# A transformer block on one core: the written-out order of its 4663 steps, and the engine of 320 of them, replaced

## The chip, the core and the metric

The kernel runs on one NeuronCore of a Trainium2 chip. Five engines work side by side, each through its own queue, in the order in which the program issues: TensorE (PE in the profile; its weight loads are PEld) multiplies matrices into PSUM, VectorE (DVE) and ScalarE (ACT) work elementwise on SBUF and PSUM, GpSimd (POOL) works elementwise on SBUF, and SyncE (SP) issues the transfers. [...] The metric is the device time of one execution in microseconds; the median of three runs is 767.39.

## The reference

One block with 2048 tokens of width 512, in float32: a layer normalization, causal attention with 32 heads of width 16 in a sliding window of 256, the output projection and the residual; then a layer normalization, a gated unit of inner width 1376 with a sigmoid gate, and the residual.

```python
q, k, v = qkv[0], qkv[1], qkv[2]                       # layernorm(x) @ wqkv
scores = jnp.einsum("bhqd,bhkd->bhqk", q, k) * (Dh ** -0.5)
mask = (idx[:, None] - idx[None, :] >= 0) & (idx[:, None] - idx[None, :] < W)
p = _softmax(jnp.where(mask[None, None], scores, -1e9), axis=-1)
o = jnp.einsum("bhqk,bhkd->bhqd", p, v)
h = x + o.transpose(0, 2, 1, 3).reshape(B, S, D) @ wo
z = _layernorm(h)
h2 = h + (_sigmoid(z @ w_gate) * (z @ w_up)) @ w_down
```

## The kernel before

**Numbers in two halves.** Every matrix product takes float16 operands, each split into a high half (a rounded copy) and a low half (the rest); a product is three matmuls, high by high, high by low, low by high. Making halves is most of the elementwise work: a high half is a copy (`copy`, L353 to L359, on ScalarE L355 or VectorE L357 and L359), a low half is a subtraction (`subtract`, L361 and L362, on GpSimd or VectorE). Weights are first scaled by a power of two found from their absolute maximum (`bound`, L364 to L369, then `scale`).

**Attention.** The tokens go in 8 blocks `b` of 256. For a block: two normalizations (`do_ln`, `normal`, L551 to L575), the projections (`do_qk`, `do_v`), copies of the keys and queries through DRAM into the stacked tiles `SK` and `SQ` (`do_keys` L677, `do_queries` L686), and for each of 8 groups `g` of four heads: scores for the row maxima (`do_s`, matmuls L740, maxima on VectorE L725), the maxima carried into two rows of `SQ` (`do_m`, L747 to L756), transposed scores with the maximum already subtracted (`do_st`, L794 to L805), their exponentials on ScalarE (L770), the masks on GpSimd (L778, L783), and products with the values (`do_pv`, L831). Then follow a transposition and an add (`do_o`, L861), the division and the output projection (`do_wo`, L873 to L899).

**The gated unit.** The tokens go in 8 pairs `p` of tiles, the inner width in three chunks `c` of 512, 512 and 352. Both sides of the products use a Strassen scheme: seven products in place of eight (`do_pair`, matmuls L1140), with sums taken of weights (`do_weights`, `do_split`, L988 to L1049 and L954, L956), of the normalized input (`do_ln2`, L1104 to L1123) and of the results. A pair's products are copied or added out of PSUM (`copied`, L357 and L355; `added`, L1161, L1163), go through the sigmoid (L1206) and the multiplication with the up side (`gated`, L1210), then four sums (`sum_`, L1224), and for four rows `r` of the hidden value a high half (`row`, through L355 or L357), a low half (through L362) and a transposition by DMA (L1240). The down products (`do_down`, L1317, L1323) read those rows; their results are added to the residual (L1288, L1300) and stored (L1294).

**What sets the order.** Each of these pieces is a Python generator. At each `yield` it names the engines that could do its next step, with a cost, and what must be done before; the step's instructions are issued when the generator goes on. `Planner.run` (L312) takes the next step from the list `ORDER` (L61 to L283): each number holds the root piece (the number without its low 7 bits), the piece among those which that root has added (the next 5 bits), and the engine (2 bits: 0 VectorE, 1 ScalarE, 2 GpSimd), used where the step leaves a choice. Costs are not used to choose anything here, nor is `Port`, which only marks steps within SBUF. So the list alone sets the order in which each engine's queue, SP's too, is filled, and which buffer of a ring (`RINGS`, L342) a step takes.

```python
        for code in ORDER:
            self.now = self.roots[code >> 7]
            item = self.now[code >> 2 & 31]
            costs, needs, *more = item[1]
            self.on = next(iter(costs)) if len(costs) == 1 else ENGINES[1 + (code & 3)]
```

Of the kernel before, what the change touches and what calls it, by code (L numbers as in the profile page):

```python
# [61 lines left out]
    3203, 3331, 771, 899, 1027, 1155, 7424, 2179, 2435, 7808, 7426, 1411, 7424, 641, 2051, 7810, 7424, 641, 1539, 7424, 1667, 7808, 641, 7427, 7808,  # L62
    3459, 7810, 1795, 641, 2307, 6658, 640, 7424, 3587, 643, 7811, 640, 2691, 3075, 641, 7808, 2947, 640, 641, 2819, 640, 641, 8323, 640, 641, 8323,
    640, 8323, 1280, 1281, 1921, 8323, 1921, 3715, 8195, 1281, 1280, 1920, 8323, 13056, 1921, 8323, 8323, 8323, 1280, 12672, 13058, 1283, 8321, 8195,
    8195, 1280, 8195, 3843, 12674, 8195, 2561, 8195, 1920, 7042, 8320, 8195, 8195, 1281, 1923, 8193, 1280, 8451, 2561, 2560, 8192, 1281, 1280, 1281,
    8579, 9219, 1280, 1281, 2561, 3971, 8451, 9219, 1280, 8451, 8835, 12672, 8579, 6018, 1920, 8835, 12673, 8451, 13056, 9219, 1921, 8451, 12672,
    8451, 4099, 1921, 8451, 18304, 8451, 8963, 8579, 1922, 8449, 8579, 8963, 2560, 8579, 1921, 8448, 8579, 8835, 6274, 8579, 1921, 13056, 8579, 8963,
    17920, 12675, 13058, 8577, 2563, 12673, 8576, 17922, 1920, 1921, 8707, 13059, 18306, 7683, 8707, 1920, 13057, 1920, 7683, 1921, 8067, 1920, 8067,
    1920, 7683, 17920, 49667, 8067, 23168, 17921, 4227, 8067, 17920, 8707, 7683, 50691, 8064, 7681, 51075, 2560, 9091, 17923, 18304, 13443, 8707,
    2561, 13443, 23552, 13443, 2561, 13443, 17921, 13443, 18304, 4355, 23554, 13443, 18304, 13443, 6402, 9091, 13443, 28416, 13571, 13441, 13571,  # L70
    6530, 9091, 13571, 10371, 10371, 13571, 10372, 10376, 6786, 13571, 13440, 13571, 13571, 13571, 10371, 10371, 10371, 13569, 10384, 23170, 13699,
    10388, 13699, 50688, 2562, 13699, 10380, 49665, 13699, 13568, 13699, 13699, 13699, 13699, 23168, 10371, 10371, 14467, 10371, 13697, 13827, 10392,
    10400, 13827, 4483, 9347, 10396, 13827, 9348, 14211, 13827, 13696, 9347, 9347, 9347, 13827, 14083, 9352, 13827, 9360, 10883, 14211, 9356, 13827,
    10884, 13827, 28800, 14211, 18307, 13825, 10883, 9347, 10883, 18305, 9364, 10888, 13824, 9347, 10883, 2561, 9368, 18691, 13955, 10892, 33664,
    18691, 2561, 14083, 9347, 18691, 23169, 18691, 14467, 9372, 9347, 18691, 10896, 23170, 13955, 18819, 9376, 9603, 18691, 14467, 9604, 10883, 10883,
    9603, 10900, 18691, 10904, 51203, 9608, 18691, 23552, 10883, 9603, 9603, 18689, 18819, 10908, 4611, 9616, 18819, 10883, 9612, 18819, 10912, 18819,
    18688, 18819, 18819, 13955, 9603, 9603, 18819, 9603, 50435, 2560, 2561, 18817, 18947, 51331, 18947, 9620, 9624, 14339, 18947, 9628, 51073, 18947,
    18816, 14083, 9603, 18947, 2561, 18947, 14339, 18947, 2562, 18947, 50179, 9632, 11139, 10115, 19075, 18945, 10116, 10115, 11140, 19075, 10120,
    13955, 2561, 6146, 11139, 11139, 19075, 11144, 11148, 19075, 2561, 18944, 11139, 7170, 10115, 19075, 10115, 11152, 19075, 10128, 19075, 14339,
    10124, 11139, 12931, 11156, 34048, 28418, 11139, 10115, 10115, 19075, 12931, 19073, 10136, 11160, 12931, 10132, 51201, 19072, 11139, 11139, 10115,  # L80
    12931, 11164, 11168, 10140, 10115, 13315, 12929, 10144, 50433, 12416, 11651, 11651, 11651, 13315, 11652, 11656, 12419, 11660, 11651, 13315, 11664,
    11907, 11907, 13315, 11908, 11912, 0, 11651, 11651, 11651, 18563, 13313, 11668, 11672, 12419, 11676, 51329, 11651, 11907, 11907, 11680, 23171,
    11916, 18563, 49411, 11920, 23169, 23552, 19203, 11907, 11907, 11907, 18563, 11928, 23554, 19203, 11924, 11932, 11907, 16387, 16387, 11936, 9475,
    9475, 18563, 33666, 16388, 9477, 9481, 16392, 16387, 28802, 16387, 18561, 9475, 16396, 16387, 9475, 6914, 9485, 12544, 16387, 9489, 23555, 16400,
    12547, 16404, 9475, 23553, 16387, 18179, 16408, 28416, 16387, 9497, 15619, 16412, 9475, 4739, 18179, 16416, 50177, 50051, 15620, 15619, 9731,
    24195, 9501, 12547, 15624, 15619, 15619, 24195, 9733, 15628, 28417, 15619, 9731, 15632, 9731, 24195, 19203, 9741, 15636, 15619, 24195, 9737,
    15640, 15619, 15619, 9731, 15644, 9731, 9745, 24195, 15648, 9753, 15363, 9750, 9731, 15364, 15363, 24195, 9757, 19331, 9506, 15368, 10243, 16899,
    15363, 24195, 10245, 16900, 9494, 10243, 10243, 15372, 9859, 16899, 10249, 16899, 9762, 24195, 10253, 38912, 50049, 15363, 10243, 28418, 10243,
    9859, 10257, 16908, 10265, 16904, 7298, 49409, 15376, 16899, 28800, 10243, 15363, 16912, 16899, 10269, 10499, 4867, 18179, 15380, 50819, 9857,
    16916, 10499, 10274, 15363, 18179, 19331, 10501, 15384, 10505, 9856, 10499, 15363, 18177, 16899, 14851, 10499, 15388, 10509, 24323, 28419, 10513,  # L90
    16920, 10499, 14852, 10518, 15363, 10499, 10521, 16899, 15392, 24323, 10262, 50563, 16924, 10525, 14851, 16899, 24323, 14856, 19331, 50817, 14851,
    11011, 16928, 10530, 24323, 19459, 11013, 14851, 14860, 24323, 39296, 11011, 10627, 14851, 19459, 11011, 14851, 10627, 11021, 28801, 49795, 14872,
    19459, 11017, 14864, 28802, 24193, 14868, 11011, 9987, 11011, 11025, 14851, 24192, 24323, 11033, 2562, 11011, 14876, 14851, 14595, 11037, 28803,
    11267, 14880, 24323, 14595, 11030, 14596, 11269, 11267, 14595, 10625, 14600, 11267, 24323, 34050, 11273, 14604, 14595, 14595, 11277, 11042, 14608,
    11267, 11281, 11267, 14612, 14595, 11289, 11267, 11286, 14616, 14595, 11395, 14595, 19587, 10624, 11293, 11779, 17155, 14620, 11781, 10755, 11779,
    11298, 14624, 11785, 11779, 17155, 24321, 17664, 17155, 11395, 17156, 11789, 17667, 49793, 24320, 17160, 11779, 17164, 17155, 24451, 11779, 11793,
    17168, 19843, 24451, 11801, 11779, 11798, 19844, 17155, 19843, 11805, 17172, 12035, 17155, 17667, 19848, 12037, 12035, 11810, 19843, 17176, 12041,
    12035, 17155, 19852, 12045, 19587, 12035, 17155, 17180, 12049, 12035, 19843, 11393, 17184, 12035, 12054, 19843, 19856, 12061, 19715, 19843, 19860,
    19843, 12057, 29443, 19715, 11392, 12163, 20867, 29443, 19864, 19715, 12066, 29443, 14723, 19587, 19843, 33664, 14723, 14725, 12163, 19868, 51843,
    33665, 19872, 4995, 14729, 20868, 20867, 50561, 14723, 20872, 20867, 14723, 14733, 29443, 20876, 20867, 14737, 20867, 29443, 20880, 14723, 12161,  # L100
    20884, 20867, 14742, 14723, 14749, 20867, 24067, 20892, 20867, 14753, 24067, 20888, 14979, 24067, 12160, 14981, 14758, 24067, 20896, 14979, 9986,
    16131, 24067, 44160, 14985, 14979, 14746, 16131, 11523, 29443, 14989, 14979, 16132, 16131, 29443, 16136, 14993, 14979, 16140, 16131, 16131, 15005,
    24067, 14998, 16144, 14979, 16148, 16131, 16131, 15009, 15491, 16152, 29443, 15002, 16156, 15493, 20099, 24067, 15014, 20100, 15491, 20099, 15491,
    10754, 20104, 20099, 16131, 24067, 16160, 20099, 12291, 15107, 15107, 24065, 29440, 20108, 17792, 15501, 20112, 17795, 15497, 29440, 51840, 20099,
    15105, 15491, 49539, 20116, 15491, 20099, 15505, 23939, 20120, 23939, 15517, 17795, 12288, 15491, 20099, 11520, 20611, 15521, 20611, 15747, 15514,
    20612, 23939, 49923, 15749, 20124, 15747, 15510, 23939, 20616, 15753, 20099, 15747, 20128, 20611, 20611, 15757, 15526, 15747, 20620, 23939, 15761,
    15104, 20611, 15747, 23939, 20624, 15773, 15747, 15770, 20611, 20628, 23939, 19203, 15777, 15766, 7552, 20611, 16259, 24064, 20611, 15875, 16259,
# [1392 lines left out]
```

## Time and profile before

| | |
|---|---|
| runs, us | 767.39, 767.2, 770.11 |
| median, us | 767.39 |
| the profiled execution: span, us | 769.3 |
| mean granted TensorE clock | 0.989 |
| busy PE, DVE, ACT, POOL, us | 729.6, 692.9, 436.9, 256.7 |
| instructions PE, DVE, ACT, POOL | 7030, 2067, 774, 319 |
| moved by DMA, MB | 118.57 |

The span runs from the first to the last instruction of the profiled execution. Busy time is the time in which at least one instruction of the engine was under way. A matmul's end is modelled and its latency counts, so PE can be busy throughout and still not be at its peak. The groups of instructions give count, busy time, mean duration of one, and the idle time of the engine just before them with what ended it.

### The profile page before, as it was taken

How to read it: one execution, taken by the hardware profiler on the slowest of the kernel's cores; microseconds unless marked ns; L12 is line 12 of the kernel's file. 1: busy time of each engine (PE TensorE's matmuls, PEld its weight loads, DVE VectorE, ACT ScalarE, POOL GpSimd, SP SyncE). 2: the span in 40 equal slices, each digit the busy share in tenths (PEclk: the TensorE clock that was granted, in tenths of full speed). 3: DMA queues.
4: the chain of work that ended last, by engine and by line, in shares of the span. 5: the costliest groups of instructions: out<-in, count | busy, mean ns of one | idle time of the engine just before them, and what ended most of it. 6: DMA issues, size and time to landing. Idle time of an engine off the chain costs nothing.

```text
span 769.3 us, 19057 instructions
## 1 busy us (share of the span) xinstructions
PE 729.6 (95%) x7030; PEld 502.0 (65%) x7030; DVE 692.9 (90%) x2067; ACT 436.9 (57%) x774; POOL 256.7 (33%) x319
## 2 busy tenths in 40 slices
PE   4899999999999999999999898699999999999997
PEld 3586678777686687686666554367565666666476
DVE  8999999978899999999998579999998989989973
ACT  5755788878688888798877667653222111121210
POOL 3333445535545466554757442240000000000000
PEclk9999999999999999999999999899999999999999
DMA  8586593886747989569587879455375665736535
GB/s 300 156 221 168 142 180 80 152 198 144 165 95 172 205 211 182 166 156 245 150 162 180 211 187 274 117 119 105 79 136 95 117 131 106 150 66 109 96 83 155
DMA packets 210318, 118.57 MB, mean 154 GB/s; under 512 B 174576, under 2 KB 183792, under 8 KB 210224
## 3 DMA queue, kind: packets, MB, share of 16 engines
q1 hardware_dynamic: 210224, 117.35, 67.9%
q8 instruction: 55, 0.90, 0.5%
q14 instruction: 39, 0.32, 0.2%
HBM read 43.65 MB, written 19.40 MB: 82 GB/s over the span
## 4 chain that ended last, share of the span: by engine, by line
PE 75%; DVE 11%; DMA 5%; issue 5%; ACT 3%; SPq 0%; DVEq 0%; ACTq 0%
PE mmp L402 18%; PE sp L1140 14%; PE mmp L1317 11%; PE pvp L831 7%; PE sp L740 6%; PE stp L1140 6%; PE pvp L1140 3%; PE stp L805 2%; PE stp L795 2%; DVE junk L725 2%; PE stp L794 1%; PE mmp L1323 1%; PE stp L796 1%; DMA oT<-whl 1%; ACT pa L770 1%
## 5 line engine op out<-in xcount | busy, mean ns | idle before, releaser
L725 DVE CUSTOM_DVE_ANT_0 junk<-sp,mask 128x320 uint8<-128x320 f32 (+4 forms) x512 | 215.4, 465 | 16.6 <-PE sp L740 14.0
L770 ACT ACTIVATE pa<-stp,kappa 128x512 f32<-128x512 f32 (+1 forms) x256 | 157.3, 645 | 48.0 <-PE stp L796 44.5
L1140 PEld LDWEIGHTS <-x 128*128 128x128 f16 x1008 | 98.3, 98 | 94.6 <-issue 10.1
L740 PE MATMUL sp<-SK,SQ 96*128 96x256 f16 (+3 forms) x960 | 129.6, 233 | 6.3 <-DVE mq L725 3.1
L402 PE MATMUL mmp<-xT,W 128*128 128x256 f16 x768 | 114.3, 281 | 3.3 <-DVE sq L661 1.7
L740 PEld LDWEIGHTS <-SQ 96*128 96x128 f16 x960 | 80.5, 97 | 30.9 <-issue 12.8
L1140 PE MATMUL sp<-W,x 128*128 128x512 f16 (+1 forms) x420 | 90.1, 351 | 6.5 <-ACT SQ L355 5.8
L770 ACT ACTIVATE pb<-stp,kappa 128x512 f32<-128x512 f32 x128 | 84.6, 685 | 19.7 <-PE stp L805 15.9
L402 PEld LDWEIGHTS <-W 128*128 128x128 f16 x768 | 71.4, 100 | 16.1 <-DVE W L539 2.9
L778 POOL TENSOR_SCALAR_AFFINE_SELECT pa<-pa 128x1024 f32<-128x1024 f32 x56 | 62.9, 1127 | 53.9 <-ACT pa L770 50.3
L831 PE MATMUL pvp<-pa,VT 128*17 128x128 f32 (+1 forms) x1408 | 62.5, 307 | 0.0
L795 PE MATMUL stp<-SQ,SK 100*128 100x256 f16 x224 | 60.2, 272 | 0.0
L563 POOL TENSOR_TENSOR rs<-rs,nhalf 128x1 f32<-128x1 f32 x32 | 20.2, 634 | 118.2 <-DVE rs L560 105.0
L783 POOL TENSOR_SCALAR_AFFINE_SELECT pa<-pa 128x512 f32<-128x512 f32 x64 | 42.6, 669 | 45.3 <-ACT pa L770 45.0
L1206 ACT ACTIVATE SQ<-sp,cg 128x512 f32<-128x512 f32 (+1 forms) x22 | 14.0, 636 | 76.6 <-PE sp L1140 76.3
L796 PE MATMUL stp<-SQ,SK 100*128 100x128 f16 x256 | 55.5, 219 | 0.7 <-ACT pb L770 0.4
L783 POOL TENSOR_SCALAR_AFFINE_SELECT pb<-pb 128x512 f32<-128x512 f32 x64 | 42.0, 658 | 42.6 <-ACT pb L770 40.1
L402 PE MATMUL mmp<-WO,oT 128*128 128x512 f16 x192 | 51.4, 389 | 2.5 <-DMA oT<-whl 2.5
L831 PEld LDWEIGHTS pvp<-pa,VT 128*17 128x17 f32 x1408 | 37.8, 97 | 22.7 <-issue 2.7
L362 DVE TENSOR_TENSOR SQ<-SQ,SQ 128x512 f16<-128x512 f32 (+3 forms) x93 | 50.2, 555 | 1.9 <-ACT SQ L355 1.3
L794 PE MATMUL stp<-SQ,SK 100*128 100x128 f16 x224 | 49.5, 221 | 1.3 <-DMA SQ<-mt 0.3
L805 PE MATMUL stp<-SQ,SK 100*128 100x256 f16 x256 | 48.1, 272 | 2.5 <-ACT pa L770 2.1
(226 smaller groups left out, 1445.8 us busy)
## 6 DMA issues: line engine op xcount, KB each, us to landing
SQ<-sq SPq DMA_DIRECT2D x96, 128.0 KB
wr<-chunk SPq DMA_DIRECT2D x28, 256.0 KB
SK<-mem SPq DMA_DIRECT2D x16, 384.0 KB
chunk<-in_wd_dram SPq DMA_DIRECT2D x20, 256.0 KB
X<-in_x_dram SPq DMA_DIRECT2D x16, 256.0 KB
mem<-sk SPq DMA_DIRECT2D x8, 512.0 KB
out_dram<-X SPq DMA_DIRECT2D x16, 256.0 KB
W<-wr SPq DMA_DIRECT2D x7, 512.0 KB
```

The lines of the kernel that those rows point to most:

```text
L402: PE.matmul(ps, a_of(a, k), b_of(b, k), start=(k == 0 and i == 0), stop=(k == n - 1 and i == 2))
L725: V.tensor_tensor_reduce(out=junk[:, c0:], in0=ps[:, c0:], in1=mask[:, c0:], scale=1.0, scalar=-3.0e38, op0=ALU.add, op1=ALU.max, accum_ou ...
L740: PE.matmul(ps[:, col:col + k1 - k0], q, SK[0:96, (2 * a + hf) % 5, 4 * (p % 2) + j, k0:k1], start=True, stop=True)
L770: S.activation(dst, a, AF.Exp, scale=kappa)
L778: G.affine_select(out=f, in_=f, pattern=[[0, 8], [-1, 128]], compare_op=ALU.is_gt, fill=0.0, base=0, channel_multiplier=1)
L783: G.affine_select(out=p, in_=p, pattern=[[0, 4], [1, 128]], compare_op=ALU.is_ge, fill=0.0, base=0, channel_multiplier=-1)
L795: PE.matmul(a[:, 128:384], ks(k0 + 1, g, j), qs(b, g, j, 0, 256), start=True, stop=True)
L796: PE.matmul(a[:, 384:512], ks(k0 + 3, g, j), qs(b, g, j, 128, 256), start=True, stop=True)
L805: PE.matmul(a[:, u, :], ks(k0 + 2, g, j + u), qs(b, g, j + u, 0, 256), start=True, stop=True)
L831: PE.matmul(ps[32 * j:32 * j + 17, u, q0:q1], VT[:, kt % 6, 8 * j + g, :], w[:, j, c:c + q1 - q0], start=first, stop=last, skip_group_chec ...
L1140: PE.matmul(ps, X2[p % 2][part][:, (a * COUNT[part] + at) * 2 + k, :], operand(c, j)[:, b, k, :], start=first and k == 0 and i == 0, stop= ...
L1317: PE.matmul(ps, hT[p, c, r][:, a, half * kinds[c] + i, :], W["d"][2 * c + i][:, b, j, :], start=fresh and c == 0 and i == 0 and n == 0, st ...
```

## The change

Only the list `ORDER` is replaced. It has 4663 numbers in both versions and runs the same generators to their end, so the same matmuls, transfers and elementwise operations are issued, in another order, and some elementwise ones on another engine. The first and last lines:

```diff
 ORDER = [
-    3203, 3331, 771, 899, 1027, 1155, 7424, 2179, 2435, 7808, 7426, 1411, 7424, 641, 2051, 7810, 7424, 641, 1539, 7424, 1667, 7808, 641, 7427, 7808,
-    3459, 7810, 1795, 641, 2307, 6658, 640, 7424, 3587, 643, 7811, 640, 2691, 3075, 641, 7808, 2947, 640, 641, 2819, 640, 641, 8323, 640, 641, 8323,
...
+    3203, 7427, 7427, 7427, 771, 643, 899, 3331, 1027, 7425, 1155, 6659, 7811, 1411, 1539, 7811, 7424, 643, 643, 7811, 7808, 7810, 643, 643, 7427,
+    1281, 1667, 643, 7424, 7811, 1281, 643, 7808, 643, 643, 2051, 8323, 1795, 2179, 3459, 643, 643, 643, 643, 643, 3587, 643, 8323, 8323, 8195, 8323,
...
+    62211, 62211, 62227, 62211, 62211, 62231, 62211, 62211, 62211, 62231, 62235, 62235,
 ]
```

Read by the numbering above, the steps that have a choice are spread over the engines so (VectorE / ScalarE / GpSimd):

| step | before | after |
|---|---|---|
| sums of the hidden value (L1224) | 91 / - / 5 | 48 / - / 48 |
| low halves of the hidden rows (L362) | 93 / - / 3 | 48 / - / 48 |
| high halves of the hidden rows (L355, L357) | 68 / 28 / - | 30 / 66 / - |
| gate multiplications (L1210) | 48 / - / 0 | 30 / - / 18 |
| copies of products out of PSUM | 49 / 23 / - | 21 / 51 / - |
| sums of the second normalization (L1122) | 30 / - / 2 | 20 / - / 12 |
| maxima of gate, up and down weights | 16 / 19 / - | 8 / 27 / - |
| maxima of the projections' weights | 4 / 8 / - | 0 / 12 / - |
| adds after the value products (L861) | 17 / - / 15 | 14 / - / 18 |
| division of the attention output (L875) | 7 / - / 9 | 2 / - / 14 |

In all 320 steps change their engine: 155 from VectorE to GpSimd, 20 back, 112 from VectorE to ScalarE, 33 back. Of the 1729 PE steps some 1016 keep their relative order; the median step moves by two places in PE's queue. VectorE's queue is reordered most: the median step that stays on it moves by 45 places. On SP's queue the first loads are now the first tile of `x`, two parts of the query weights, the second tile of `x`, the other query weights and then the key weights; before, they were both tiles of `x`, the query weights, two parts of the value weights and then the key weights. The change is described as an order and choice of engines searched anew, in which VectorE's steps within SBUF exclude every pending GpSimd step, with durations taken from two traces.

437 rows, old and new, of the table ORDER are left out of this document.

## The prediction

> **What bounds the kernel now.** I read the stretches of time first, then the chain that ended last, then the waits, then the groups of instructions. The stretches are cut where the list of steps has the same matrix product in both versions at nearly the same amount of matrix work done: the value projection of the first block (38 us), the last product of probabilities and values (455 us), the fifth of the seven products of pair 1, chunk 1 (502 us), the last product (765 us). Columns: length, then busy time of PE, PE weight loads, DVE, ACT, POOL with their counts, PE clock, DMA share, GB/s.
>
> ```profile
> 0.00:38.00 38.00, 25.23 (x159) 16.42 (x160) 33.55 (x77) 24.82 (x49) 13.22 (x28) 0.96 0.71 226
> 38.00:455.00 417.00, 405.11 (x4932) 295.77 (x4931) 377.22 (x1372) 323.24 (x564) 215.65 (x260) 1.00 0.75 171
> 455.00:502.00 47.00, 37.24 (x185) 18.26 (x184) 46.41 (x91) 32.01 (x59) 10.03 (x8) 0.89 0.80 205
> 502.00:765.00 263.00, 261.59 (x1757) 171.42 (x1756) 235.01 (x529) 56.88 (x104) 17.81 (x23) 1.00 0.56 109
> 765.00:769.30 4.30, 0.40 (x4) 0.11 (x2) 0.75 (x1) 0.00 (x0) 0.00 (x0) 0.95 0.27 101
> ```
>
> PE is idle 12.8, 11.9, 9.8, 1.4 and 3.9 us, 39.8 in all: that is all the visible room. In the fourth stretch PE is never short of work, so nothing that another engine saves there can shorten it. In the first and third, DVE is busy 33.55 of 38 and 46.41 of 47 us while PE waits. The second is mixed: PE's busy time overstates its work there, because short matmuls are counted with their latency.
>
> ```profile
> 15.09 1.78 DVE am L369 x3
> 460.15 3.88 DMA oT<-whl
> 489.10 0.99 DVE W L1026 x2
> 490.09 1.32 DVE WD L956 x2
> 491.75 1.46 DVE W L1026 x2
> 541.66 1.29 PE sp L1140 x6
> 222.67 2.72 PE pvp L831 x64
> ```
>
> From the chain (start, length, what): in the first stretch the absolute maxima of weights on DVE (`am`) are on it; in the third it is weight splitting on DVE (`W`, `WD`); in the fourth PE alone, six matmuls of 512 columns in 1.29 us, 0.215 each. Counting the second stretch's matmul columns at that rate, and its value products at 2.72 us each, gives about 385 us of matrix work in 417: an estimate of 32 us of room, 20 more than the idle time shows.
>
> ```profile
> PE sp L1140 <- ACT SQ L355: 6.4, 2, 5.8
> PE sp L740 <- DVE mq L725: 3.1, 6, 1.2
> PE mmp L402 <- DMA oT<-whl: 2.5, 2, 2.1
> PE sp L740 <- DMA SK<-mem: 1.6, 1, 1.6
> PE mmp L1317 <- DMA RH<-SQ: 0.8, 1, 0.8
> ...
> ACT W L537 <- DVE sq L388: 2.0, 1, 2.0
> ```
>
> PE's waits (total us, times, longest): the 5.8 us is at 490 us, where ACT itself waited for DVE. No single wait of the second stretch is over 2.1 us: it loses by many small ones.
>
> **The change, part by part.** No instruction of the computation is added or removed; the list gives the same 4663 steps another order, and 320 of them another engine: 155 go from VectorE to GpSimd and 20 back, 112 from VectorE to ScalarE and 33 back. The lists read by their code numbers give, before and after, on VectorE: sums of hidden blocks 91 to 48 and their low halves 93 to 48, gates 48 to 30 (all these to GpSimd); high halves 68 to 30, copies of products 49 to 21, maxima of weight chunks 16 to 8 and of the projections' weights 4 to 0 (these to ScalarE). Durations, with the mean in ns behind the comma:
>
> ```profile
> L1224 DVE TENSOR_TENSOR SQ<-SQ 128x256 f32<-128x256 f32 (+1 forms) x91 | 34.7, 389 | 0.8
> L362 DVE TENSOR_TENSOR SQ<-SQ,SQ 128x512 f16<-128x512 f32 (+3 forms) x93 | 50.2, 555 | 1.9 <-ACT SQ L355 1.3
> L1210 DVE TENSOR_TENSOR SQ<-SQ 128x512 f32<-128x512 f32 (+1 forms) x48 | 29.8, 630 | 6.2 <-ACT SQ L1206 5.6
> L357 DVE CAST SQ<-SQ 128x512 f16<-128x512 f32 (+3 forms) x68 | 23.6, 353 | 0.7 <-DMA RH<-SQ 0.2 <-DMA oT<-SQ 0.2
> L357 DVE COPY SQ<-sp 128x512 f32<-128x512 f32 (+1 forms) x18 | 11.5, 639 | 11.2 <-PE sp L1140 11.2
> L355 ACT ACTIVATE SQ<-SQ 128x512 f16<-128x512 f32 (+3 forms) x28 | 14.3, 529 | 27.7 <-DMA OS<-SQ 9.5 <-DVE SQ L1224 9.3 <-DVE SQ L1210 6.3
> L1224 POOL TENSOR_TENSOR SQ<-SQ 128x128 f32<-128x128 f32 (+1 forms) x5 | 4.1, 830 | 4.3 <-DVE SQ L1224 2.9 <-DVE SQ L1210 1.3
> L362 POOL TENSOR_TENSOR hl<-chunk,hl 128x512 f16<-128x512 f32 (+1 forms) x4 | 4.0, 1029 | 0.0
> L875 POOL TENSOR_TENSOR OS<-OS,rc 128x512 f32<-128x512 f32 x9 | 9.9, 1102 | 4.0 <-DVE rc L873 4.0
> L369 DVE TENSOR_REDUCE amd<-chunk 128x1 f32<-128x512 f32 (+1 forms) x7 | 4.7, 680 | 0.7 <-DMA chunk<-in_wd_dram 0.7
> L369 DVE TENSOR_REDUCE am<-wk 128x1 f32<-128x512 f32 x2 | 1.3, 678 | 0.0
> ```
>
> *Fourth stretch.* 39 sums x 0.389, 41 low halves x 0.555, 19 gates x 0.630, 38 high halves x 0.353 and 26 copies x 0.639 leave VectorE: 15.2 + 22.8 + 12.0 + 13.4 + 16.6 = 80 us of its 235. GpSimd gains 39 x 0.830 + 41 x 1.029 + 18 x 1.102 = 94 us on 17.8, ScalarE 64 x 0.53 = 34 us on 56.9. All three then stay under 160 of 263 us. PE covers all of it: worth **0**. If that cover went, it would be because a longer step on GpSimd (1.029 for 0.555) makes a tile late for PE.
>
> *First stretch.* The four maxima that leave VectorE are 4 x 0.678 = 2.7 us, three of which the chain shows at 15.09; three steps of the first normalizations move later. ScalarE takes on about 3 us; it is busy 24.8 of 38, and in this stretch it waits 2.0 us for VectorE's scale (`sq` L388, above), which covers most of that. The loads of the key weights also go ahead of two of the value weights on SP's queue. I take **-2.5**; bounds 0 (ScalarE or the loads end last) and -5.
>
> *Third stretch.* On VectorE it loses 4 low halves, 3 sums, two steps of the output projection and two pairs of weight steps: by the rows above 4 x 0.555 + 3 x 0.389 + 2 x 0.7 + some of the weight work, about 5 us of 46.4. VectorE ends last there, so I take **-5**; bounds 0 and -9.8 (all of PE's idle time).
>
> *Second stretch.* Off VectorE: 8 maxima x 0.680, four normalizations of the attention output, three adds, four sums of the second normalization and a few casts, less two copies that come back: about 13 us of 377. Neither engine is full (VectorE 90%, matrix work 92%), each waits for the other in small pieces, so I take half: **-6**; bounds 0 and -13, and the rival below for more.
>
> *New waits.* An in-order queue has the steps behind the waiting one held up: SP issues every transfer, so a transposition that waits for a GpSimd subtraction holds the loads and key copies behind it. I take **+2** spread over the tiles that now come closest; bounds 0 and +32, worked out below.
>
> The sum: 769.3 - 2.5 - 6 - 5 + 2 = 757.8 us for an execution like the profiled one. That one is 1.9 us over the median of the three (767.39), so the time is 757.8 - 1.9 = **756 us**.
>
> **VectorE and GpSimd together.** [...] The columns are min/median/max in ns:
>
> ```profile
> L747 DVE TENSOR_SCALAR mh<-mq x16: 116/176/1636, 69.0 to 417.1; 128x32 f16<-128x32 f32 x16
> L573 DVE TENSOR_SCALAR xn<-X,mv,rs x12: 447/542/1521, 36.0 to 277.6; 128x512 f32<-128x512 f32 x12
> L725 DVE CUSTOM_DVE_ANT_0 junk<-sp,mask x512: 215/485/493, 43.1 to 416.6; 128x320 uint8<-128x320 f32 x149, 128x64 uint8<-128x64 f32 x7, 128x256 uint8<-128x256 f32 x7, 128x128 uint8<-128x128 f32 x4
> ```
>
> A step of 176 ns once took 1636, and one of 542 took 1521, each about a GpSimd step longer; the row maxima, which read PSUM, never did. Taking for every step on VectorE its excess over the median of its kind, the trace holds about 29 us of such time, some 20 of it before 502 us. The new order is said to keep the two apart.
>
> [...]
>
> **The rivals.**
> - *The waits at the port vanish too.* If order alone removes the 20 us before 502 us and half of it reaches PE, 10 us more go: 746. For it: VectorE is the late one there. Against: GpSimd gets about 27 us more work in the same stretches, more chances to meet.
> - *The middle gains nothing.* If PE's small losses in the second stretch come from its own order and from ScalarE (323 us busy, and a few more), that term is 0: 762.
> - *The shared port.* If a step moved to GpSimd blocks VectorE as long as it freed it, only the moves to ScalarE count: -2.5 in the first stretch, 8 maxima x 0.680 / 2 = -2.7 in the second, +2: 769.3 - 3.2 - 1.9 = 764, no measurable change. In the fourth stretch even this is hidden: the in-SBUF steps left on VectorE are about 80 us and GpSimd's 112, 192 of 263.
> - *The order doesn't do what it says.* The list plans; the engines run when they can. If the chip's waits differ from the planned ones the relief may be spent on new ones, which ends at the same 764 to 767.
> - *Late transfers, slower.* One transposed tile took 3.98 us from issue to landing and one key copy 6.62:
>
> ```profile
> 758.25 3.98 DMA RH<-SQ
> 204.49 6.62 DMA SK<-mem
> ```
>
> In the old list the hidden tile issued closest to the product that reads it has 1.5 us of matrix work in between, the next 2.9. In the new list eleven are closer than 2.9, two have nothing in between; short of 2.9 they lack 14 us together. Key copies had at least 4.2 us; in the new list eight have less and lack 18. If list place were issue time, up to 32 us of waiting would come in. Two thirds of that on top of 756 is about 776. From about 15 us it makes the kernel slower than before. Against it: in the new list neighbouring steps stand so close that they can't all be in order of start, so the place says less than in the old one.
>
> **How the numbers follow.** Chances: forecast 756: 0.38; waits at the port vanish too, 746: 0.17; middle gains nothing, 762: 0.15; shared port or new waits, 764 to 767: 0.14; late transfers, 776: 0.16. A measurement tells from no change what differs by over 0.5%, here 3.8 us, so the first three are faster (0.70), the fourth the same (0.14), the last slower (0.16). The bounds of the terms added give -28 and +32; the range 743 to 773 leaves out the far end of the late transfers and the case that every gain comes in full, under 2 in 10.
>
> **What would show it.** Right: VectorE busy below 165 us between the same two products of the fourth stretch, and PE still idle under 3 us there; the third stretch near 42 us; the first near 35.5. The `am` pieces of 15.09 gone from the chain. Wrong: PE waits of over 1 us for hidden tiles or `SK<-mem` (late transfers); the second stretch still 417 us (middle gains nothing); in-SBUF steps of VectorE with many durations of over 1 us (shared port).

## The result: 762.38 us, and the profile after

| | before | after |
|---|---|---|
| median of nine runs each, us | 767.2 | 762.38 |
| lowest to highest, us | 765.31 to 772.08 | 761.53 to 764.52 |
| span of the profiled execution, us | 769.3 | 760.7 |
| busy DVE, ACT, POOL, us | 692.9, 436.9, 256.7 | 631.1, 474.2, 377.7 |

The ratio of after to before is 0.9926, with a 95% interval of 0.9904 to 0.9948: faster by 0.7%, 5.7 us of 767. The forecast was 756, about twice that gain. The stretches of the changed kernel, cut at the ends of the same four matrix products (columns as in the prediction):

```profile
0.00:37.30 37.30, 23.64 (x156) 15.15 (x157) 31.63 (x68) 27.33 (x58) 16.77 (x23) 1.00 0.64 224
37.30:444.70 407.40, 400.68 (x4935) 294.69 (x4933) 370.50 (x1350) 327.21 (x580) 229.51 (x283) 1.00 0.77 177
444.70:494.80 50.10, 38.04 (x185) 18.33 (x184) 49.88 (x83) 32.68 (x61) 19.26 (x18) 0.90 0.78 189
494.80:756.80 262.00, 261.61 (x1759) 171.49 (x1756) 178.32 (x353) 86.96 (x166) 112.19 (x133) 1.00 0.57 108
756.80:760.70 3.90, 0.02 (x1) 0.00 (x0) 0.75 (x1) 0.00 (x0) 0.00 (x0) 0.75 0.20 74
```

To the hundredth, the lengths to the same product's end are:

| stretch | before | after | difference | forecast |
|---|---|---|---|---|
| first | 37.75 | 37.32 | -0.4 | -2.5 |
| second | 417.08 | 407.34 | -9.7 | -6 |
| third | 47.24 | 50.16 | +2.9 | -5 |
| fourth | 263.33 | 262.00 | -1.3 | 0 |

The four and the tail, 0.0, make 8.6 us; the medians differ by 4.8. A run's time is about 1.7 us longer than its span (762.41 for 760.7 here), so by its span of 769.3 the profiled execution of before took about 771.0 us, 3.8 over the median of its nine, while that of the changed kernel lies on its median. In which stretches these 3.8 us sit is not shown. Part can be the clock: before, TensorE's granted clock was 0.51 from 24.7 to 28.1 us and 0.50 from 212.5 to 215.9, with PE busy throughout. An estimate from these figures is a loss of up to 1.7 us each time. The changed kernel has no such time in its first two stretches, and both have 10.2 us of it in the third.

So the sign of the third stretch was wrong: VectorE has eight instructions fewer there (83 for 91) and is busy longer, 49.88 of 50.10 us. The waits of PE, same columns as in the prediction:

```profile
...
PE mmp L402 <- DMA oT<-whl: 4.8, 2, 3.6
PE mmp L609 <- DVE SQ L1224: 3.1, 1, 3.1
...
PE mmp L402 <- DVE W L362: 2.0, 1, 2.0
PE sp L1140 <- ACT SQ L355: 1.8, 1, 1.8
...
PE sp L740 <- DVE mq L725: 1.4, 2, 1.0
```

The first line of the list, left out here, is the start (6.6 us, 7.0 before). The 5.8 us wait at 490 us is gone, others stand in the third stretch in its place (3.6 and 3.1 us are at 451 and 459 us). No wait for a hidden tile and none for `SK<-mem` is in the list: the late transfers of the slow rival did not come. The score products' wait for the row maxima (`mq`), spread over the second stretch, fell from 3.1 to 1.4 us.

**Where the third stretch's relief went.** Groups of VectorE's instructions in the third stretch, shapes apart (busy us, mean ns of one), before:

```profile
L956 DVE SCALAR_TENSOR_TENSOR WD<-chunk,sd,WD 128x512 f16<-128x512 f32 x10 | 7.4, 743 | 0.3 <-ACT WD L954 0.3
L1045 DVE SCALAR_TENSOR_TENSOR WD<-WD,ratio 128x352 f32<-128x352 f32 x3 | 1.6, 546 | 0.0
L362 DVE TENSOR_TENSOR WD<-WD 128x352 f32<-128x352 f32 x2 | 1.0, 516 | 0.0
```

and after:

```profile
L956 DVE SCALAR_TENSOR_TENSOR WD<-chunk,sd,WD 128x512 f16<-128x512 f32 x10 | 9.2, 925 | 0.0
L1045 DVE SCALAR_TENSOR_TENSOR WD<-WD,ratio 128x352 f32<-128x352 f32 x3 | 3.5, 1151 | 0.0
L362 DVE TENSOR_TENSOR WD<-WD 128x352 f32<-128x352 f32 x2 | 1.9, 942 | 0.0
```

The same instructions, as many of them, take longer: 9.2 us for 7.4 in the first group, 5.4 for 2.6 in the other two. To count it everywhere, I give each line, operation and shape on VectorE its usual duration (the least of its medians in four kernels: before, after and the first two experiments), and split every instruction into that and the rest, its excess. Sums in us (they are above busy time, as neighbouring records overlap by some 0.07):

| VectorE: usual + excess | first | second | third | fourth |
|---|---|---|---|---|
| before | 35.5 + 0.9 | 459.0 + 9.0 | 52.2 + 1.5 | 265.5 + 1.3 |
| after | 31.2 + 2.6 | 446.0 + 14.9 | 47.2 + 8.5 | 181.0 + 15.4 |

In the third stretch VectorE's own work fell by 5.0 us, which is the forecast's term, and 7.0 us of excess came in.

The excess is time spent waiting for GpSimd. In the changed kernel 82 instructions of VectorE took over 0.08 us more than usual, in before 27. Each of them has the end of a GpSimd instruction inside it and ends behind it by its usual duration less 0.13 to 0.40 us, as if it had only run then. In all fourteen kernels of this study it is 961 of 961 such instructions; of the other instructions of VectorE 18% have such an end inside. So VectorE waits for GpSimd also where the two instructions share no tile (below, 2.08 us in place of 0.54 for a normalization of `X` into `xn` that ends behind clears of `SQ`). I call such a wait a collision.

### The profile page after: what moved, and what is told of

It is laid out like the page before. It is cut to its first block, busy times and chain, and to the rows that moved or that the text cites. A ratio compares the mean times of both kernels' runs of the same rounds, so it can differ in the third digit from the quotient of the medians.

```text
span 760.7 us, 19217 instructions
## 1 busy us (share of the span) xinstructions
PE 724.0 (95%) x7030; PEld 499.7 (66%) x7030; DVE 631.1 (83%) x1852; ACT 474.2 (62%) x864; POOL 377.7 (50%) x456
## 4 chain that ended last, share of the span: by engine, by line
PE 74%; DVE 16%; issue 5%; ACT 2%; DMA 2%; SPq 0%; POOL 0%; DVEq 0%; ACTq 0%
PE mmp L402 15%; PE sp L1140 14%; PE mmp L1317 12%; PE pvp L831 8%; PE sp L740 7%; PE stp L1140 6%; DVE junk L725 3%; PE pvp L1140 3%; PE stp L805 3%; PE stp L795 2%; PE stp L794 1%; PE mmp L1323 1%; PE stp L796 1%; ACT pa L770 1%; DVE WD L956 1%
## 5 line engine op out<-in xcount | busy, mean ns | idle before, releaser
L725 DVE CUSTOM_DVE_ANT_0 junk<-sp,mask 128x320 uint8<-128x320 f32 (+4 forms) x512 | 215.0, 464 | 14.9 <-PE sp L740 12.5
L740 PE MATMUL sp<-SK,SQ 96*128 96x128 f16 (+3 forms) x960 | 127.9, 232 | 2.9 <-DVE mq L725 1.4
L402 PE MATMUL mmp<-xT,W 128*128 128x256 f16 x768 | 111.6, 277 | 2.9 <-DVE xT L357 0.8
L402 PEld LDWEIGHTS <-W 128*128 128x128 f16 x768 | 69.8, 98 | 16.1 <-DVE W L539 3.1
L362 POOL TENSOR_TENSOR SQ<-SQ,SQ 128x512 f16<-128x512 f32 (+3 forms) x48 | 45.4, 955 | 53.3 <-ACT SQ L355 26.6
L1224 POOL TENSOR_TENSOR SQ<-SQ 128x256 f32<-128x256 f32 (+1 forms) x48 | 35.0, 732 | 52.2 <-DVE SQ L1210 30.8
L795 PE MATMUL stp<-SQ,SK 100*128 100x256 f16 x224 | 59.7, 270 | 0.0
L355 ACT ACTIVATE SQ<-SQ 128x512 f16<-128x512 f32 (+3 forms) x66 | 33.6, 520 | 40.3 <-DVE SQ L1224 13.6
L402 PE MATMUL mmp<-W,xT 128*128 128x512 f16 x192 | 49.6, 378 | 2.2 <-DVE W L362 2.0
```

The lines of the kernel that those rows point to most:

```text
L402: PE.matmul(ps, a_of(a, k), b_of(b, k), start=(k == 0 and i == 0), stop=(k == n - 1 and i == 2))
L725: V.tensor_tensor_reduce(out=junk[:, c0:], in0=ps[:, c0:], in1=mask[:, c0:], scale=1.0, scalar=-3.0e38, op0=ALU.add, op1=ALU.max, accum_ou ...
L740: PE.matmul(ps[:, col:col + k1 - k0], q, SK[0:96, (2 * a + hf) % 5, 4 * (p % 2) + j, k0:k1], start=True, stop=True)
L795: PE.matmul(a[:, 128:384], ks(k0 + 1, g, j), qs(b, g, j, 0, 256), start=True, stop=True)
```

## The experiments

All change the list alone, except one. A number of the list holds the step and, in its last two bits, its engine; where a step leaves no choice these two bits mean nothing, and the lists differ in them.

**Order and engines apart.** The order of the change with the engines of before, and the other way round:

```diff
-    7425,   # a step of the changed order on ScalarE
+    7424,   # on VectorE, as before; and so on, all 320
```

> The steps in the order of the changed kernel, each on the engine it has before (none of the 320 moves). If the gain of the second stretch (417.0 to 406.7 us between the same products) comes from the order, that stretch stays near 407 and the time near 762 or below, since the third stretch gets back its 16 steps' old engines: 758 to 763. If the gain comes from the steps taken off VectorE, the second stretch goes back to about 415 and the time to 767 or above, as an order planned for other engines can only fit worse: 766 to 772.

> The order of before with the 320 changed engines. If the relief of VectorE is what counts, the second stretch falls to some 407 to 410 us and the time to 759 to 763. If the order counts, the second stretch stays at 415 to 417 and the time at 766 to 770. If GpSimd's added steps hold VectorE up at the port wherever nothing keeps them apart, VectorE's excess over the medians of its kinds is above the 38.7 us of the changed kernel, and the time is 768 or more.

Measured: ratios to before of 1.0574 (1.0552 to 1.0596) and 1.0193 (1.0175 to 1.0212), 813.01 and 784.58 us. The first is far from both of its expected ranges. The second falls under its last one, at 768 or more, by its number but not by its cause: it has 44.2 us of excess in all where the changed kernel has 41.4, and 2.8 us more do not explain 22 us of time. (The 38.7 us in the text above, and 6.5 in a later one, are counted over other medians than the table.) Stretches of the first:

```profile
0.00:38.93 38.93, 25.18 (x156) 15.43 (x157) 34.01 (x74) 24.64 (x49) 14.30 (x21) 0.96 0.62 215
38.93:463.45 424.52, 406.57 (x4935) 295.65 (x4933) 382.90 (x1375) 323.60 (x563) 218.97 (x267) 1.00 0.74 170
463.45:513.01 49.56, 38.09 (x185) 17.93 (x186) 49.00 (x93) 33.12 (x61) 8.67 (x8) 0.93 0.72 188
513.01:806.59 293.58, 269.33 (x1758) 172.30 (x1756) 235.38 (x527) 56.06 (x101) 17.38 (x24) 0.99 0.50 97
```

and of the second:

```profile
0.00:40.59 40.59, 26.81 (x158) 16.50 (x159) 32.98 (x78) 27.03 (x58) 15.37 (x31) 0.92 0.70 226
40.59:467.76 427.17, 409.42 (x4933) 296.17 (x4931) 372.80 (x1339) 328.92 (x580) 227.52 (x274) 1.00 0.71 165
467.76:515.72 47.96, 37.43 (x185) 18.44 (x186) 46.87 (x81) 31.77 (x59) 21.25 (x20) 0.89 0.78 204
515.72:782.70 266.98, 262.92 (x1758) 171.39 (x1756) 182.23 (x355) 88.63 (x167) 113.13 (x133) 1.00 0.57 108
```

| length, us | old order, old engines | new order, old engines | old order, new engines | both new |
|---|---|---|---|---|
| second stretch | 417.1 | 424.5 | 427.2 | 407.3 |
| third | 47.2 | 49.6 | 48.0 | 50.2 |
| fourth | 263.3 | 293.6 | 267.0 | 262.0 |

In the second and fourth stretches each half alone makes it slower; both together are faster in the second and 1.3 us apart in the fourth. Look at the fourth with old engines: VectorE has the same 235 us to do as before, in 293.6 us rather than 263.0. PE waits there for VectorE's copies and additions, 18.7 us in all (L359 8.3, L357 4.5, L1163 3.3, L1288 2.6). So not VectorE's load but the order in which things stand in the queues costs 30 us; which of the queues it is was not taken apart. A price of a moved step taken from its duration alone, as the forecast has it, says nothing of this. In the third stretch the new engines never pay: +0.7 us in the old order, +0.6 in the new one, both small beside the scatter of this stretch (below, under the first stretch).

**Where the gain sits.** The change up to the last product of probabilities and values, then before; and that with the fourth stretch of the change again:

```diff
-    first, second, third and fourth stretch of the new list
+    first and second stretch of the new list, third of the old, fourth of the old (or of the new)
```

> The changed kernel up to the last product of probabilities and values, then order and engines of before. If the changed kernel loses 3 us in its third stretch by the way that stretch is planned (its order or its GpSimd steps), the third stretch is near 47 us here and the time near 759 (762.4 - 3.1). If the 3 us are work that the second stretch left over (what was gained before the border is paid behind it), the third stretch stays at 50 or more and the time at 762 to 763. The fourth stretch 263 in both.

> Order and engines of the change in the first two stretches, those of before in the third, those of the change again in the fourth. If the stretches add up, it has the second of the changed kernel (407), the third of before (47.2) and the fourth of the changed kernel (262): 759.5 for an execution whose changed kernel takes 762.4, and no slower than the kernel with both last stretches of before (759.9 on its chip). If the fourth stretch's moves cost anything, it is above that one.

Measured: 759.9 us, ratio 0.9885 (0.9867 to 0.9903), and 760.26 us, 0.9877 (0.985 to 0.9904). The third stretch is 47.34 and 46.73 us, the second stays at 407 to 408. So the third stretch's loss is made in its own order and engines and is not work left over from the second, and the 203 engine moves of the fourth stretch, nearly two thirds of all, are worth nothing that can be measured: 263.02 us with the old order and engines, 263.29 with the new ones.

**What slows the third.** Its 16 moves undone, in the new order:

```diff
-    58026,  # a sum (S1) on GpSimd
+    58024,  # on VectorE; and 15 more between the borders of the stretch, three of them to GpSimd
```

> The changed kernel with the 16 steps of the third stretch that change engine (sums, low halves, weight steps, mostly GpSimd) back on their engines of before. If collisions with GpSimd's steps are what eats that stretch, VectorE's excess over the medians falls there from 6.5 us to about 2 and the stretch to 46 or 47: time 758 to 759. If VectorE's plain work is the bound, the returned steps (about 5 us) lengthen the stretch to 53 to 55: time 765 to 767. If the late transposition of the attention output is the bound (the wait of 3.58 us for it), neither matters: 762 to 763.

Measured: 763.74 us, 0.9938 (0.9919 to 0.9956), as the changed kernel itself. By its time the third explanation, the late transposition, would stand. The split of VectorE's time speaks against it: 52.6 + 3.6 us where the changed kernel has 47.2 + 8.5. Both other causes were at work, 5.4 us returned and 4.9 saved, and left 49.56 us. To part them, the collisions have to go without the work coming back:

```diff
...
-    V, S, G, PE = nc.vector, nc.scalar, nc.gpsimd, nc.tensor
+    V, S, G, PE, short = nc.vector, nc.scalar, nc.gpsimd, nc.tensor, lambda v: v[:, :16] if plan.on == POOL_ and 3385 <= plan.n < 3596 else v
...
-        (G if plan.on == POOL_ else V).tensor_tensor(out=out, in0=a, in1=b, op=ALU.subtract)
+        (G if plan.on == POOL_ else V).tensor_tensor(out=short(out), in0=short(a), in1=short(b), op=ALU.subtract)
...
```

The sum (`sum_`, L1224) is cut the same way, and `plan.n` is the place in the list.

> The changed kernel, with 16 column-wise steps of GpSimd in the third stretch (low halves L362 and sums L1224 behind the first three of the stretch) computing only 16 of their columns: that part of the hidden blocks and of the last projection's weights is left out. VectorE's own steps, the order and every transfer stay. If VectorE ends last in this stretch and loses its relief by waiting for GpSimd's steps at the port, its excess over the usual durations falls there from 8.5 us to 3 or less and the stretch from 50.2 to 44 to 46 us. If the stretch is set by its order (the late transposition, the normalization queued behind weight steps), the excess falls but the stretch stays at 48 to 50.

(It is 14 steps, not 16, that are cut; their other columns are missing from the result.) Measured: 756.16 us, 0.983 (0.981 to 0.9851). The third stretch, and the three groups in it:

```profile
443.81:487.07 43.26, 35.87 (x185) 17.64 (x186) 43.04 (x83) 32.37 (x61) 10.39 (x18) 0.96 0.90 219
```

```profile
L956 DVE SCALAR_TENSOR_TENSOR WD<-chunk,sd,WD 128x512 f16<-128x512 f32 x10 | 7.4, 742 | 0.0
...
L362 DVE TENSOR_TENSOR WD<-WD 128x352 f32<-128x352 f32 x2 | 1.9, 953 | 0.0
...
L1045 DVE SCALAR_TENSOR_TENSOR WD<-WD,ratio 128x352 f32<-128x352 f32 x3 | 1.7, 579 | 0.0
```

Same order, same 83 instructions on VectorE, same transfers: 50.2 us becomes 43.3, and the split is 47.2 + 1.8. Two of the three groups are back at their durations of before; in the third, one instruction still took 1.39 us, behind GpSimd's multiplication L875 (455.52 to 456.90 us), which was left whole. The transposition still comes late and PE waits even longer for it,

```profile
PE mmp L402 <- DMA oT<-whl: 4.9, 2, 4.2
```

but the stretch is short all the same: that wait lies inside VectorE's time. VectorE is busy 43.04 of 43.26 us here and 46.65 of 47.24 before. Its 83 instructions lost 6.7 us of excess, and the stretch 6.9. TensorE's clock differs too (at half for 3.4 us in this stretch, 10.2 in the changed kernel), but VectorE is busy throughout both and PE idle for 7.4 and 12.1 us, so PE is not the one that sets the length. The collisions are shown as the cause. Without them the change gives 43.3 us, where the forecast had 42.

**The first stretch.** VectorE's instructions (start, length) in the changed kernel:

```profile
30.28 0.69 DVE L362 TENSOR_TENSOR W<-wv,W 128x512 f16<-128x512 f32 x1
...
31.49 0.68 DVE L362 TENSOR_TENSOR W<-wv,W 128x512 f16<-128x512 f32 x1
32.09 2.08 DVE L573 TENSOR_SCALAR xn<-X,mv,rs 128x512 f32<-128x512 f32 x1
...
35.08 1.59 DVE L362 TENSOR_TENSOR W<-wv,W 128x512 f16<-128x512 f32 x1
```

and GpSimd's:

```profile
30.34 3.54 POOL L516 MEMSET SQ<- 32x2048 f32 x2
34.97 1.15 POOL L362 TENSOR_TENSOR hl<-xn,hl 128x512 f16<-128x512 f32 x1 [1.09 <-ACT hl L355]
```

The normalization (L573) ends 0.29 us behind GpSimd's clears, the subtraction behind GpSimd's subtraction: 1.5 and 0.9 us over their usual 0.54 and 0.69. PE's 2.0 us wait for `W L362` follows at once. Only the clears were moved:

```diff
     1921,
-    7171,   # clear
     2561,
...
     4099,
-    6787,   # clear
...
     9603,
+    7170,
+    6786,
```

> The changed kernel with two clearing steps of GpSimd (L516, 3.54 us together from 30.34 to 33.88) moved from there to about 49 us, where GpSimd is idle; nothing else differs. In the changed kernel the normalization L573 took 2.08 us in place of 0.54 and ended just behind them, and PE then waited 2.03 us for a weight piece behind it on VectorE. If VectorE was held up by the two clears, L573 takes about 0.54 here, the wait of 2.03 us is under 0.7, the first stretch is about 35.8 (37.3 before this edit) and the time 1 to 1.5 us less than that of the changed kernel. If the first stretch is set by something else (loads, ScalarE), the stretch stays at 37 and the time within 0.5 us.

Measured: 758.72 us, 0.9866 (0.9834 to 0.9899). The same stretch of VectorE's time line:

```profile
31.99 0.55 DVE L573 TENSOR_SCALAR xn<-X,mv,rs 128x512 f32<-128x512 f32 x1
...
33.45 0.68 DVE L362 TENSOR_TENSOR W<-wv,W 128x512 f16<-128x512 f32 x1
```

Both are back at their usual durations, the second at 33.45 us, 1.63 us earlier than in the changed kernel, where GpSimd's subtraction ran from 34.97; the first stretch is 35.0 us, VectorE's part 31.4 + 0.2. Two numbers of 4663 were worth 2.3 us in the profile's first stretch. (The ratio to before, 0.9866 for the changed kernel's 0.9926, is 4.6 us better and is not all accounted for. The profiled execution, 763.35 us, is the longest of its six, with 53.0 us in the third stretch: there the granted clock was 0.50 from 488.2 to 495.0 us, just ahead of the product that ends the stretch, where the changed kernel has 1.00. So one order of this stretch can differ by 2.8 us between executions. The loss in it is still clear: the four kernels with the new third stretch have 50.2 to 53.0 us, the four with that of before 46.7 to 47.6.)

**The second stretch, by engine.** The 40 moves between VectorE and GpSimd ahead of the third stretch undone, and, in another kernel, the 61 between VectorE and ScalarE:

```diff
-    17922,  # a low half on GpSimd
+    17920,  # on VectorE; 40 steps put back, 11 of them to GpSimd
-    1281,   # a maximum on ScalarE
+    1280,   # on VectorE; 61 steps put back in the other kernel, 23 of them to ScalarE
```

> The changed kernel with the 40 moves between VectorE and GpSimd ahead of the third stretch undone, both ways; the moves between VectorE and ScalarE stay. If steps moved to GpSimd cost VectorE about what they free (as the third stretch has it: 5.0 us freed, 7.0 us added by collisions), VectorE's collisions in the second stretch fall from 14.9 towards 9 us and the time stays at 761 to 764. If they are relief at their face value (the 27 to 13 us of the forecast), the second stretch lengthens by 5 to 8 us: 767 to 771.

> The changed kernel with the 61 moves between VectorE and ScalarE ahead of the third stretch undone, both ways; the moves to and from GpSimd stay. If ScalarE's share is the relief that counts, the second stretch lengthens by 6 to 10 us and the time is 768 to 772, clearly above the run with GpSimd's moves undone. If only the fit of order and engines counts, whichever part is undone, both are slower by about the same. If neither matters, 762 to 764.

Measured: 768.41 us, 0.998 (0.9958 to 1.0002), and 780.13 us, 1.0132 (1.0098 to 1.0166). The second stretch has 411.1 and 422.3 us. GpSimd's moves there are worth 3.8 us: without them VectorE has 454.4 + 14.0, with them 446.0 + 14.9. So 8.4 us of work left for 0.9 of excess: here the relief is real, at the half that the forecast took. ScalarE's moves are worth 14.9 us for 5.3 us of VectorE's work and 2.5 of its excess (451.3 + 17.4 without them). Load alone can't be why; the waits of that kernel say more:

```profile
PE sp L740 <- DVE mq L725: 8.3, 15, 1.4
```

1.4 us of waiting for the row maxima became 8.3. The order alone and the engines alone have the same wait, 8.5 and 7.9 us. A reading that fits, though no run shows which steps do it: a step put back on VectorE stands in the queue ahead of a maximum that PE needs. The rest of the 14.9 us is spread over small waits.

**A version that beats both.** Old third stretch, the rest new, clears later; then two tries to shorten the third further:

```diff
     56737,
+    56356,   # the weight step that PE needs
     56364,
...
+    57617, 56237, 56236, 57492, 57603, 57500, 57504, 57624, 57509, 57508, 57511, 57731,
     56456,   # weight splits that nothing needs yet
-    56237,
     56736,
...
```

> The kernel with the third stretch of before and the rest of the change, and the two clearing steps moved to 49 us. If the two repairs add up, 760.3 - 2.3 = 758 us. If the later clears collide with something else there, 760.

> The last one, and near the end of its third stretch: the weight splits of the down projection that nothing needs before 499 us (L956) go behind the steps that the third chunk's products wait for, on VectorE; ScalarE's copy of the product (L355) goes ahead of the weight steps that it stood behind; PE takes the second product of the down projection two products later. In the kernel with the third stretch of before PE waits 6.8 us there. If VectorE's work of the third stretch can be paid in the fourth, where the change has freed it (181 of 262 us busy), the third falls by 3 to 5 us and the time to 753 to 755. If the waits only move to the next product, within 1 us of the last one: 757 to 759.

> The deferred kernel, with two of its new waits taken away: VectorE's additions and sums for the third and second chunk (L1161, L1163, L1224) ahead of the weight splits that wait for ScalarE (VectorE was idle 1.65 us there, and PE then waited 3.73 us for L1161), and the second product of the down projection two products later again. If VectorE's work of the third stretch can be paid in the fourth, the third stays near 41 and the fourth falls from 271 to 265 or less: time 752 to 755. If what is deferred always comes back as a wait of PE for the next hidden block, it stays within 2 us of the repaired kernel without deferral, 756 to 760.

Measured: 757.57 us, 0.985 (0.983 to 0.9869); 759.04, 0.9881 (0.9859 to 0.9903); 760.98, 0.9911 (0.9889 to 0.9933). The first is the fastest kernel of this study that computes the whole result, with twice the change's gain, from putting one stretch back and moving two steps:

```profile
0.00:34.59 34.59, 22.49 (x156) 14.71 (x157) 29.47 (x69) 27.21 (x58) 11.89 (x20) 1.00 0.67 237
34.59:442.00 407.41, 400.59 (x4935) 294.61 (x4933) 370.33 (x1348) 327.50 (x580) 233.88 (x286) 1.00 0.76 177
442.00:489.58 47.58, 37.03 (x185) 18.04 (x186) 47.51 (x93) 32.30 (x60) 10.21 (x9) 0.93 0.79 194
489.58:751.93 262.35, 261.76 (x1758) 171.51 (x1756) 178.65 (x352) 87.33 (x167) 113.11 (x133) 1.00 0.57 109
```

Deferring gained nothing. The third stretch did fall, the fourth took it back; the last two stretches of the first try:

```profile
440.87:482.00 41.13, 33.90 (x180) 16.56 (x180) 40.50 (x78) 26.90 (x50) 7.76 (x7) 1.00 0.76 185
482.00:753.01 271.01, 264.94 (x1764) 172.48 (x1762) 185.62 (x366) 92.75 (x176) 115.64 (x136) 0.99 0.58 112
```

6.5 us gained (0.65 of it a product of PE that was moved over the border), 8.7 lost. PE was idle 5.5 us more, by this wait among others, and busy 3.2 us longer: 0.65 for what was moved, and the granted clock was 0.50 from 487.4 to 494.2 us, a time at half clock that the kernel without deferral has at 480.7 to 487.5, inside its third stretch:

```profile
PE pvp L1140 <- DVE SQ L1161: 3.7, 1, 3.7
```

With it taken away, the second try has a longer one, one product on:

```profile
PE sp L1140 <- ACT SQ L355: 8.3, 3, 7.1
```

Whether VectorE's work at the end of the third stretch can be paid in the fourth, where it has 80 us free, stays open: what two orders made by hand show is only that they don't do it.

## Why the prediction was right and wrong

- *Direction and mechanism.* Faster, as forecast; by relief of VectorE only in part, since the same engines in the old order are 1.9% slower. The size was off: 762.4 for 756. The rival "the middle gains nothing" had 762 too, and is wrong: the middle gained most. Luck has a share: by the profiles the second stretch came out 3.7 us better than forecast and the third 7.9 us worse, and the sum hides both.
- *Fourth stretch, 0.* Right, and shown: 263.0 and 263.3 us with the old and new halves, behind the same start. That VectorE would be busy under 165 us there was wrong, 178.32: its own work fell by 84.5 us, near the 80 of the rows, but 14.1 us of excess came in, hidden by PE, and the rows took the overlap of neighbouring records off busy time too, some 14 us for 176 instructions.
- *Second stretch, -6.* 9.7 us. The count of VectorE's relief, "about 13 us", was right to the microsecond (459.0 to 446.0), "half" was right for GpSimd's moves (3.8 of 8.4) and far too low for ScalarE's (14.9 for 5.3). The rule that a step is worth a share of its duration failed there: 6.9 of the 14.9 us are the longer waits for row maxima. That PE lost its time there by many small waits was right.
- *Third stretch, -5.* This is the step that failed: "VectorE ends last there, so I take -5; bounds 0 and -9.8". VectorE does end last, and 5.0 us left it. The bounds left out that steps put on GpSimd make VectorE's other steps longer: 7.0 us of excess. The term was right, and another, of the other sign, was missing.
- *First stretch, -2.5.* The same: 4.3 us of VectorE's work left, two collisions of 2.4 us in all came on the path, -0.4 remained. Without them it is 35.0 us for the 35.3 that the forecast's term gives. As forecast, the pieces of `am` at 15 us are off the chain; ScalarE's weight halves are on it (start, length, what):

```profile
20.26 2.45 ACT W L537 x4
```

- *Collisions.* The prediction took the change's aim, to keep the two engines apart, as an upper side only ("the waits at the port vanish too"). They went the other way: 12.7 us of excess in all before, 41.4 after (the rows of the table). Its "about 29 us" was too large: grouped by line, operation and names, with shapes mixed, the trace of before gives 29.3; with shapes apart it gives 15.4, of which 13.6 are ahead of 502 us, not 20. The rival of the shared port had the cause, but as "a step moved to GpSimd blocks VectorE as long as it freed it", everywhere and with a chance of 0.14. By stretch it is true in the third (7.0 for 5.0), false in the second (0.9 for 8.4, by the moves put back) and in the fourth (14.1 for 84.5). Nor is it the moves alone: the new order with the old engines has 15.0 us of excess in the second stretch, where before has 9.0, and 3.7 in the third for 1.5. The change is described as an order that keeps the two apart; on the chip they meet three times as often. That the place of the wait is a port, as two of the rivals call it, no run shows; what the runs show is the 961 instructions that end just behind one of GpSimd's.
- *New waits, +2; late transfers.* The transfers were no cost, as the prediction's argument against them had it. SP's queue did stand for GpSimd's low halves (`SPq L1240 <- POOL SQ L362`), 40.1 us in 15 waits after, the longest 5.0, where before has 4.2 us in two; but 38.7 of the 40.1 are behind 500 us, in the fourth stretch, where PE was idle 0.4 us in all. The one transposed tile that PE waits 3.6 us for in the third stretch lies within VectorE's time, as the shortened steps show.

Which of VectorE's steps take part shows in the first stretch: beside the clears, which read no tile, the subtractions with two inputs took 0.69 and 0.68 us, and beside a subtraction of GpSimd, which does read, 1.59. The normalization, with one input, took 2.08 beside the clears. In all fourteen traces 49 instructions of VectorE were held up beside a clear, and each has one input.

## What to carry to other kernels

Where VectorE was busy without a break, its relief counted nearly in full (4.0 us of 5.0 in the third stretch, once the collisions were gone). But price a step moved from VectorE to GpSimd twice: once for what leaves the queue, once for how much longer the rest of that queue gets (5.0 and 7.0 us in the third stretch), and let the bounds reach to the other sign. An order and a choice of engines fit each other or don't: each half of this change alone lost 2% to 6%, so neither can be judged or copied alone. Cut both traces at the same products: a stretch that lost can then be put back whole. Here that took the ratio from 0.9926 to 0.9877, and two clears moved as well to 0.985.

## What the hardware showed beyond that

Which steps of VectorE get longer is sharply drawn. In the changed kernel (min/median/max in ns, first and last start):

```profile
L556 DVE BATCH_NORM_STATS2 st<-X x32: 637/684/695, 3.6 to 671.9; 128x6 f32<-128x512 f32 x32
```

```profile
L899 DVE SCALAR_TENSOR_TENSOR X<-mmp,co,X x16: 735/744/750, 151.3 to 483.8; 128x512 f32<-128x512 f32 x16
```

```profile
L573 DVE TENSOR_SCALAR xn<-X,mv,rs x12: 542/776/2076, 32.1 to 269.0; 128x512 f32<-128x512 f32 x12
```

The statistics of the normalization, one SBUF tile in and a few numbers out, and the additions with one input in PSUM never went over their median by more than 11 ns, in stretches where other steps of VectorE took two to four times theirs. Over all fourteen kernels the 7168 scans for the row maxima, the 448 statistics and the 224 additions of L899 were never 0.08 us over their usual durations, though a GpSimd step ended inside 2216, 161 and 92 of them. The sums of the second normalization (L1122), with two inputs in SBUF, were over it 54 of the 55 times that one did. What a clear of only 32 partitions costs was not expected either: it held the normalization of 128 partitions for 1.5 us.
